# Squares of the activations taken from PSUM, a planner that costs one kind of matmul lower, and three small constants in one tile

## The chip, the core and the metric

The kernel runs on one core of one Trainium2 chip. The engines are named as in the profile: PE is TensorE's matmul (PEld its weight load), DVE is VectorE, ACT is ScalarE, POOL is GpSimd and SP is SyncE, whose queue issues nearly all DMAs. Each engine works through its own queue in order and waits there for semaphores of the others. The metric is the time on the device of one execution, in microseconds. Between the profiled execution's own time and the span that the profile shows from the first to the last instruction lie about two microseconds.

## What is computed

Two blocks with adaptive layer norm, over 2048 rows of 512 values, in float32. The first is a convolution of length 2048 for each of 512 channels, whose kernel comes from 128 complex poles; the second is a dense layer of 1792 units with a squared rectifier. Cut to what matters:

```python
def _A_ref(u, A_re, A_im, B_re, B_im, C_re, C_im, log_dt, Dskip):
    ...
    K = einsum("dn,dnl,dn->dl", Cc, exp(dt * A * l), dB).real
    y = irfft(rfft(pad(u)) * rfft(pad(K)))[:L] + u * Dskip
    return y

def _B_ref(x, w1, b1, w2, b2):
    h = x @ w1 + b1
    r = where(h > 0, h, 0)
    return (r * r) @ w2 + b2

mod = silu(c) @ w_mod                       # sa, ca, ga, sb, cb, gb
h = layernorm(x) * (1 + ca) + sa
x = x + ga * _A_ref(h, ...)
h = layernorm(x) * (1 + cb) + sb
x = x + gb * _B_ref(h, ...)
```

## The kernel before

It has two halves. Up to about 293 us, it makes the convolution in eight chunks of 64 channels: tables and transforms of the kernel, transforms of the input, products, and a first inverse step, whose result lies in the two big tiles `big0` and `big1`. After it come the second inverse step, the second layer norm and the dense layers.

**The second inverse step** (`inverse`, matmuls at L980) has four parts, n = 0 to 3, and each gives four tiles of 128 rows (s = 4n to 4n+3; tiles count from 0 to 15). A part has 256 small matmuls of 32 x 32 weights and 128 columns, as the profile counts them. Parts 0 and 2 write the two `tg` tiles of PSUM, parts 1 and 3 the four banks `ps0` to `ps2` and `kg`. Part 0 is emptied by DVE (L989), the others by ACT (L991), and for these POOL then adds the residual (L994).

**The layer norm** takes, for each tile, statistics on DVE (`statistics`: L1000, L1001), a square root on ACT (L1002), its reciprocal on DVE (L1003). `prepare` then scales the tile: for the first four tiles L1010 on DVE makes the negated mean times the reciprocal and L1012 on ACT scales, for the others L1014 on DVE does all of it. Four transposes on PE (L1021) put the tile into a bank, ACT (L1028, one quarter) and DVE (L1024, three quarters) modulate it, ACT (L1032) rounds it to the matmul's fast format and DVE or POOL (L1034) takes the rest, so that the sum of two rounded parts stands for the float32 value. L1017 and L1060 add the last bias to the residual on POOL.

**The dense layers** run over four groups of four tiles with 14 blocks of 128 units each, 56 steps in all. Step i has 12 matmuls of the first layer into one of the four banks (L1084, L1085, L1087: high by high, low by high, high by low) and 12 of the second layer of step i-2 into the `tg` tiles (L1104, L1105, L1106). Between them lie four instructions: the rectifier with its bias on ACT (L1090), the square on ACT, rounded (L1091), the square on DVE in full (L1092) and the difference of both (L1093), which is the low part. `w2_split` brings the second layer's weights, through two buffers of a quarter tile, and splits them (L929 on ACT, L930 on POOL).

**What sets the order.** The kernel is written down once, and `keep_order` then sets the order of every engine's queue: it runs the recorded instructions through a small model in which `weight` gives each a duration, takes on each engine the ready one with the longest way to the end, and fixes that order by dependencies. It models PE at half speed when the last window of 3413 ns was not busy enough (`level`), and lets DVE and POOL wait for each other where `shares_port` says that both use SBUF's shared port. So a change of one duration moves work in the second half, and the real times of the instructions don't change by it. The matmuls of inverse parts 0 and 1 and of the dense layers keep their written turn (`in_turn`); parts 2 and 3 and the first four tiles' transposes may move.

Of the kernel before, what the change touches and what calls it, by code (L numbers as in the profile page):

```python
# [11 lines left out]
F32 = mybir.dt.float32  # L12
FR = mybir.dt.float32r
I32 = mybir.dt.int32
AF = mybir.ActivationFunctionType
ALU = mybir.AluOpType
# [90 lines left out]
def weight(ins):  # L107
# [3 lines left out]
    if "DMA" in type(ins).__name__:  # L111
# [10 lines left out]
            if cols == 32 and ins.ins[1].ap[0][1] == 32:  # L122
                return 42, 42 + 130
            tiles = 128 // cols if cols in (32, 64, 128) else 1
# [28 lines left out]
def keep_order(tc, traced, slots, in_turn, whole, urgent, behind):  # L153
# [104 lines left out]
    for _ in groups:  # L258
# [7 lines left out]
        if e == "PE":  # L266
            kind = free_size(groups[g][0].ins[1]) if len(groups[g][0].ins) > 1 else shape
            cost += 0 if kind == shape else 230 if shape == 32 else 110
            shape = kind
            cost /= level(now)  # L270
            a = now
            while a < now + cost - 1:
                w = int(a // WINDOW)
                b = min(now + cost, (w + 1) * WINDOW)
                busy[w] = busy.get(w, 0) + b - a
                a = b
        elif e == "DVE":
            port = shares_port(groups[g][0])
            cost += max(0, free["Pool"] - now) if port else 0
        elif e == "Pool":  # L280
            cost += max(0, free["DVE"] - now) if port else 0
        elif e == "Activation":
            new = function_table(groups[g][0]) or table
            cost += 1283 if new != table else 0
            table = new
# [20 lines left out]
def tile_adaln_ssm_ffn(  # L306
# [60 lines left out]
    halfpi = ctile("halfpi", [P, 1])  # L367
    tiny = ctile("tiny", [P, 1])
    rsq = ctile("rsq", [P, 4])
    cin = ctile("cin", [P, 4])  # L370
# [78 lines left out]
    make_identity(nc, ident)  # L449
    pick, second = ctile("pick", [P, 128], FR), ctile("second", [P, 1])  # L450
    firsts = ident.rearrange("p (q a) -> p a q", q=4)
# [553 lines left out]
    def prepare(s):  # L1005
# [3 lines left out]
        if s < 4:  # L1009
            nc.vector.scalar_tensor_tensor(  # L1010
                mv[:, s, 1:2], mv[:, s, 0:1], -1.0, rstd2[:, s : s + 1], op0=ALU.mult, op1=ALU.mult)
            nc.scalar.activation(d4(xn), x2[:, s], AF.Identity, scale=rstd2[:, s : s + 1], bias=mv[:, s, 1:2])  # L1012
# [63 lines left out]
    def ffn1(i):  # L1076
# [14 lines left out]
        nc.scalar.activation(r2h, rr, AF.Square)  # L1091
        nc.vector.tensor_mul(rr, rr, rr)  # L1092
        nc.vector.tensor_sub(r2l, rr, r2h.bitcast(F32))  # L1093
        r2[i] = r2h, r2l
# [82 lines left out]
```

## Time and profile before

| | us |
|---|---|
| median of three runs | 655.47 |
| the three runs | 650.13, 655.47, 662.59 |
| the profiled execution, its own time | 654.19 |
| its span, first to last instruction | 652.1 |

| engine | busy us | share of the span |
|---|---|---|
| PE | 594.2 | 91% |
| PEld | 509.1 | 78% |
| DVE | 379.2 | 58% |
| ACT | 347.7 | 53% |
| POOL | 303.0 | 46% |

The mean granted clock of PE was 0.976 of full speed. On the chain of work that ended last, PE has 77% of the span, ACT 6%, DVE 5%, POOL 4%, waits that the profile cannot name 4%, and DMA 3%. These shares are means over the two halves, which have different limits: the first half uses all engines, the second is nearly PE alone. In the views below a row of the order of time has start, length, engine, line, operation, tiles, shape and count, and in brackets the idle time of the engine before it with what ended it. "issue" stands there where the engine waited for nothing that the profile shows. Rows that overlap were merged where they follow each other.

### The profile page before, as it was taken

How to read it: one execution, taken by the hardware profiler on the slowest of the kernel's cores; microseconds unless marked ns; L12 is line 12 of the kernel's file. 1: busy time of each engine (PE TensorE's matmuls, PEld its weight loads, DVE VectorE, ACT ScalarE, POOL GpSimd, SP SyncE). 2: the span in 40 equal slices, each digit the busy share in tenths (PEclk: the TensorE clock that was granted, in tenths of full speed). 3: DMA queues.
4: the chain of work that ended last, by engine and by line, in shares of the span. 5: the costliest groups of instructions: out<-in, count | busy, mean ns of one | idle time of the engine just before them, and what ended most of it. 6: DMA issues, size and time to landing. Idle time of an engine off the chain costs nothing.

```text
span 652.1 us, 20850 instructions
## 1 busy us (share of the span) xinstructions
PE 594.2 (91%) x9322; PEld 509.1 (78%) x9322; DVE 379.2 (58%) x646; ACT 347.7 (53%) x648; POOL 303.0 (46%) x251
## 2 busy tenths in 40 slices
PE   2389997999999999897769999999999999999995
PEld 2267886999899899885658888888888888888884
DVE  5797778899699789454596532533325332252223
ACT  4957999898997768433745532244322433222220
POOL 5489699999999996078976200011000100000000
PEclk9979999999999999997879999999999999999998
DMA  8932014032022405572141000100001000010001
GB/s 321 376 132 66 4 36 96 8 68 55 17 68 60 124 4 149 137 271 68 55 150 59 2 0 1 64 1 0 2 1 64 1 1 1 0 65 1 0 1 64
DMA packets 21705, 42.30 MB, mean 65 GB/s; under 512 B 3696, under 2 KB 9200, under 8 KB 20336
## 3 DMA queue, kind: packets, MB, share of 16 engines
q1 hardware_dynamic: 21184, 40.84, 20.3%
q8 instruction: 73, 1.20, 0.8%
q10 hardware_dynamic: 432, 0.14, 0.1%
q14 instruction: 16, 0.13, 0.1%
HBM read 28.39 MB, written 4.19 MB: 50 GB/s over the span
## 4 chain that ended last, share of the span: by engine, by line
PE 77%; ACT 6%; DVE 5%; POOL 4%; issue 4%; DMA 3%; SPq 0%; DVEq 0%; POOLq 0%; ACTq 0%
PE tg L1104 8%; PE tg L1105 8%; PE tg L1106 8%; PE ps L671 7%; PE ps L681 7%; PE ps L828 7%; PE ps L1085 6%; PE ps L1084 6%; PE ps L1087 6%; PE kg L809 4%; PE ps L634 3%; PE kg L1085 2%; PE kg L1084 2%; PE kg L1087 2%; ACT tables L756 1%
## 5 line engine op out<-in xcount | busy, mean ns | idle before, releaser
L1092 DVE TENSOR_TENSOR xy<-xy 128x512 f32<-128x512 f32 x56 | 45.8, 818 | 163.1 <-ACT rw L1091 106.4
L1090 ACT ACTIVATE xy<-ps,b1c 128x512 f32<-128x512 f32 x42 | 28.9, 689 | 134.5 <-PE ps L1087 134.5
L1017 POOL TENSOR_TENSOR big<-big,lo 128x512 f32<-128x512 f32 x12 | 16.0, 1332 | 158.5 <-DVE xy L1014 158.5
L681 PE MATMUL ps<-xy,t_sb 128*64 128x64 f32 x2048 | 66.7, 223 | 5.6 <-issue 3.3
L681 PEld LDWEIGHTS ps<-xy,t_sb 128*64 128x64 f32 x2048 | 63.5, 138 | 7.9 <-issue 3.6
L828 PE MATMUL ps<-e_sb,xy 128*64 128x128 f32 x1024 | 62.0, 274 | 2.8 <-issue 2.3
L828 PEld LDWEIGHTS ps<-e_sb,xy 128*64 128x64 f32 x1024 | 56.6, 138 | 4.7 <-issue 3.2
L673 ACT COPY xy<-ps 128x512 f32<-128x512 f32 x64 | 37.1, 591 | 15.3 <-PE ps L671 14.9
L789 POOL TENSOR_TENSOR rtl<-tables 128x1024 f32<-128x1024 f32 x22 | 43.4, 1971 | 0.2
L819 DVE TENSOR_TENSOR xy<-ps,xy 128x512 f32<-128x512 f32 x64 | 39.8, 680 | 2.0 <-PE ps L681 1.6
L1084 PE MATMUL ps<-h0h,w1h 128*128 128x512 f32 x88 | 35.3, 401 | 0.5 <-ACT big L991 0.5
L834 DVE COPY big<-ps 128x256 f32<-128x256 f32 x64 | 24.1, 417 | 19.8 <-PE ps L828 19.8
L765 POOL TENSOR_TENSOR llph<-lo,big 128x1024 int32<-128x1024 int32 x16 | 34.7, 2169 | 0.7 <-ACT tg L777 0.7
L765 POOL TENSOR_TENSOR rtl<-lo,big 128x1024 int32<-128x1024 int32 x16 | 34.3, 2142 | 1.5 <-ACT tg L777 1.0
L671 PE MATMUL ps<-d_sb,ksb 128*64 128x128 f32 x512 | 33.9, 275 | 1.1 <-DVE xy L819 0.8
L1090 ACT ACTIVATE xy<-kg,b1c 128x512 f32<-128x512 f32 x14 | 9.7, 690 | 47.1 <-PE kg L1087 42.8
L671 PE MATMUL ps<-d_sb,big 128*64 128x128 f32 x512 | 31.6, 274 | 0.8 <-ACT big L637 0.7
L1084 PE MATMUL ps<-h,w1h 128*128 128x512 f32 x80 | 31.6, 395 | 0.0
L1093 DVE TENSOR_TENSOR rw<-xy,rw 128x512 fp32r<-128x512 f32 x37 | 28.6, 774 | 2.9
L671 PEld LDWEIGHTS ps<-d_sb,ksb 128*64 128x64 f32 x512 | 28.1, 137 | 2.5 <-DVE xy L819 1.0
L671 PEld LDWEIGHTS ps<-d_sb,big 128*64 128x64 f32 x512 | 28.4, 137 | 1.6 <-ACT big L637 1.0
L800 DVE TENSOR_TENSOR rtl<-rtl,tg 128x1024 f32<-128x1024 f32 x22 | 26.7, 1213 | 2.4 <-POOL rtl L789 2.4
(260 smaller groups left out, 1604.0 us busy)
## 6 DMA issues: line engine op xcount, KB each, us to landing
xy<-xt SPq DMA_DIRECT2D x32, 256.0 KB, 4.4
xy<-xy SPq DMA_DIRECT2D x16, 512.0 KB, 6.2
xy<-w_mod SPq DMA_DIRECT2D x6, 1024.0 KB, 8.4
out_dram<-xy SPq DMA_DIRECT2D x16, 256.0 KB, 2.1
xy<-w SPq DMA_DIRECT2D x14, 256.0 KB, 3.1
raw<-w SPq DMA_DIRECT2D x6, 512.0 KB, 6.3
t_sb<-c_t SPq DMA_DIRECT2D x1, 2048.0 KB, 11.6
i2c<-c_i SPq DMA_DIRECT2D x1, 2048.0 KB, 8.5
```

The costliest lines, as they stand in the source:

```text
L671: nc.tensor.matmul(ps[64 * r : 64 * r + 64, 128 * i : 128 * i + 128], src[:, i], d1_sb[:, r], start=True, stop=True)
L681: nc.tensor.matmul(ps[64 * r : 64 * r + 64, 64 * i : 64 * i + 64].rearrange("p (h q t) -> p q h t", h=2, t=2), t2_sb[:, 8 * g + i, r], src ...
L765: nc.gpsimd.tensor_tensor(ph.rearrange("p d r (a b) -> p (d r) a b", a=4), bc(low_phase[:, us].rearrange("p d r b -> p (d r) b"), 2, 4), b ...
L789: nc.gpsimd.tensor_mul(am[:, 0, :, 32:96].rearrange("p d (v x) -> p d v x", v=2), bc(et[:, 256 + 8 * d0 : 384 + 8 * d0].rearrange("p (y a) ...
L828: nc.tensor.matmul(ps[64 * m : 64 * m + 64, 128 * i : 128 * i + 128], pairs(y)[:, g, i // 2, 64 * m : 64 * m + 64, i % 2], e1_sb[:, h], st ...
L1084: pe.append(nc.tensor.matmul(ps, w1h[:, q, fs], hh[:, q, :], start=(q == 0), stop=False))
L1085: pe.append(nc.tensor.matmul(ps, wl[:, q], hh[:, q, :], start=False, stop=False))
L1087: pe.append(nc.tensor.matmul(ps, w1h[:, q, fs], hl[:, q, :], start=False, stop=(q == 3)))
L1092: nc.vector.tensor_mul(rr, rr, rr)
L1104: pe.append(nc.tensor.matmul(acc, r2l[:, ms], hi_, start=(t == 0), stop=False))
L1105: pe.append(nc.tensor.matmul(acc, r2h[:, ms], lo_, start=False, stop=False))
L1106: pe.append(nc.tensor.matmul(acc, r2h[:, ms], hi_, start=False, stop=(t == NF - 1)))
```

## The change

Three things. Three small constants, of one, four and one columns, become views of one tile of eight columns, which moves the large tiles at the left side of SBUF by 64 bytes. In the dense layers, the square on DVE is taken as (bank + bias) times the rectified tile and written back into the bank in PSUM, and the low part is then the bank less the rounded square; before, it was the rectified tile times itself, in SBUF. In the planner, the small inverse matmul costs 24 ns instead of 42, and at least three quarters of the full clock are assumed for it. L1010 is written as one operation with two scalars, with the same result.

```diff
             if cols == 32 and ins.ins[1].ap[0][1] == 32:
-                return 42, 42 + 130
+                return 24, 24 + 130
...
-            cost /= level(now)
+            cost /= max(level(now), 0.75 if kind == 32 and groups[g][0].ins[1].ap[0][1] == 32 else 0)
...
-    tiny = ctile("tiny", [P, 1])
-    rsq = ctile("rsq", [P, 4])
+    small = ctile("small", [P, 8])
+    tiny, rsq, second = small[:, 0:1], small[:, 1:5], small[:, 5:6]
...
-    pick, second = ctile("pick", [P, 128], FR), ctile("second", [P, 1])
+    pick = ctile("pick", [P, 128], FR)
...
-            nc.vector.scalar_tensor_tensor(
-                mv[:, s, 1:2], mv[:, s, 0:1], -1.0, rstd2[:, s : s + 1], op0=ALU.mult, op1=ALU.mult)
+            nc.vector.tensor_scalar(
+                mv[:, s, 1:2], mv[:, s, 0:1], rstd2[:, s : s + 1], -1.0, op0=ALU.mult, op1=ALU.mult)
...
-        nc.vector.tensor_mul(rr, rr, rr)
-        nc.vector.tensor_sub(r2l, rr, r2h.bitcast(F32))
+        nc.vector.scalar_tensor_tensor(ps, ps, b1c[:, t : t + 1], rr, op0=ALU.add, op1=ALU.mult)
+        nc.vector.tensor_sub(r2l, ps, r2h.bitcast(F32))
```

The order of every engine stays as it was up to the second inverse step. Behind it, three places matter. In the names, the numbers behind the tiles only count tiles and differ between the two programs; `ps_160` of before is `ps_158` of after, `big_84` and `big_85` are `big_83` and `big_84`.

PE, from the end of inverse part 1 to the start of part 3. Before (a quarter of part 2 is four rows, eight matmuls in each):

```order
L980 MATMUL tg_427<-big_85,i2c 32x128 x8
L980 MATMUL tg_428<-big_85,i2c 32x128 x8
L1021 MATMUL ps_160<-ident,xy_92 128x128 x4
L1021 MATMUL ps_161<-ident,xy_92 128x128 x4
L980 MATMUL tg_427<-big_84,i2c 32x128 x8
L980 MATMUL tg_428<-big_84,i2c 32x128 x8
L980 MATMUL tg_427<-big_85,i2c 32x128 x8
L980 MATMUL tg_428<-big_85,i2c 32x128 x8
L1021 MATMUL kg_364<-ident,xy_92 128x128 x4
L1021 MATMUL ps_159<-ident,xy_92 128x128 x4
```

Two quarters of part 2 follow there, and then part 3. After, the end of part 2:

```order
L980 MATMUL tg_425<-big_84,i2c 32x128 x8
L980 MATMUL tg_426<-big_84,i2c 32x128 x8
L1021 MATMUL ps_158<-ident,xy_91 128x128 x4
L1021 MATMUL ps_159<-ident,xy_91 128x128 x4
L1021 MATMUL kg_362<-ident,xy_91 128x128 x4
L1021 MATMUL ps_157<-ident,xy_91 128x128 x4
L980 MATMUL ps_157<-big_83,i2c 32x128 x4
```

The four tiles' transposes moved behind all of part 2, and part 3 follows them at once.

ACT, at the same place: the root L1002 and scaling L1012 of the first four tiles, and the copies L991 of part 1. Before:

```order
L929 CAST w_5030<-xy_96 128x512
L1002 ACTIVATE rstd_77<-mv_72,epsb 128x1
L1012 ACTIVATE xy_92<-big_84,mv_72,rstd_77 128x512
L1002 ACTIVATE rstd_77<-mv_72,epsb 128x1 x2
L991 COPY big_84<-ps_160 128x4x8x16
```

After:

```order
L991 COPY big_83<-ps_158 128x4x8x16
L1002 ACTIVATE rstd_76<-mv_71,epsb 128x1
L991 COPY big_83<-ps_159 128x4x8x16
L1002 ACTIVATE rstd_76<-mv_71,epsb 128x1
L991 COPY big_83<-kg_362 128x4x8x16
L1012 ACTIVATE xy_91<-big_83,mv_71,rstd_76 128x512 x2
L1002 ACTIVATE rstd_76<-mv_71,epsb 128x1 x2
L991 COPY big_83<-ps_157 128x4x8x16
L1012 ACTIVATE xy_91<-big_83,mv_71,rstd_76 128x512 x2
```

The copies of part 1 moved ahead of the first root, and the splitting of two weight tiles (L929) moved behind this stretch. Further on, the copies of part 3 now stand behind the roots of tiles 5 to 7.

POOL, from the end of the first layer's weights to the second layer's. Before:

```order
L930 TENSOR_TENSOR w_5020<-xy_96,w_5020 128x512
L930 TENSOR_TENSOR w_5030<-xy_96,w_5030 128x512
L1060 TENSOR_TENSOR big_84<-big_84,lo 128x4x8x16 x4
L994 TENSOR_TENSOR big_84<-big_84,xy_94 128x4x8x16 x2
L1034 TENSOR_TENSOR h0l<-xy_92,h0h 128x4x128 x4
L930 TENSOR_TENSOR w_5030<-xy_96,w_5030 128x512 x2
L994 TENSOR_TENSOR big_84<-big_84,xy_94 128x4x8x16 x4
```

After:

```order
L1060 TENSOR_TENSOR big_83<-big_83,lo 128x4x8x16 x2
L994 TENSOR_TENSOR big_83<-big_83,xy_93 128x4x8x16 x4
L1034 TENSOR_TENSOR h0l<-xy_91,h0h 128x4x128 x4
L930 TENSOR_TENSOR w_5018<-xy_95,w_5018 128x512
L930 TENSOR_TENSOR w_5028<-xy_95,w_5028 128x512
L994 TENSOR_TENSOR big_83<-big_83,xy_93 128x4x8x16 x3
```

The residual adds of tiles 4 to 7 moved ahead of L1034, two weight splits and two L1060 moved behind. On DVE, the first square L1092 stands behind the statistics of tile 10, where before it stood behind those of tile 9.

## The prediction

> **What bounds the kernel now.** I read the tenths of the page first, then the sums of PE's waits around the place that the tenths show, then the order of time there. The tenths:
>
> ```profile
> PE   2389997999999999897769999999999999999995
> POOL 5489699999999996078976200011000100000000
> PEclk9979999999999999997879999999999999999998
> ```
>
> PE, the TensorE matmul, is at 9 from the sixth slice on, and from slice 23 (358 us) without a break: the feed-forward part has no wait to give. The one weak place is slices 19 to 21, 293 to 342 us, where PE falls to 7, 6 and 9 and its granted clock to 7, 8 and 7. PE's waits between 290 and 345 us:
>
> ```profile
> PE tg L1104 <- DVE w1lc L1093: 5.7, 1, 5.7
> PE tg L980 <- issue: 2.7, 3, 1.5
> ```
>
> From 345 us on there is no wait of PE in the trace at all. The longest is one wait of 5.7 us, of the first second-layer matmul for the low half of the first square. In order of time:
>
> ```profile
> 329.81 3.77 POOL L994 TENSOR_TENSOR big<-big,xy 128x512 f32<-128x512 f32 x3
> 329.87 6.69 DVE L1092 TENSOR_TENSOR xy<-xy 128x512 f32<-128x512 f32 x1 [0.33 <-ACT w1lc L1091]
> 330.57 1.08 PE L1087 MATMUL kg<-h0l,w1h 128*128 128x512 f32 x4
> 334.71 1.30 POOL L994 TENSOR_TENSOR big<-big,xy 128x512 f32<-128x512 f32 x1
> 336.59 0.69 DVE L1093 TENSOR_TENSOR w1lc<-xy,w1lc 128x512 fp32r<-128x512 f32 x1
> 337.34 0.79 PE L1104 MATMUL tg<-w,w1lc 128*128 128x512 f32 x1 [5.69 <-DVE w1lc L1093]
> ```
>
> The square on DVE takes 6.69 us instead of some 0.68 (its row has two SBUF operands), and ends 0.55 us after POOL's last add of that run (334.71 + 1.30 = 336.01). So it stood behind POOL. PE was done at 331.65 and waits until 337.34. It then starts at half speed:
>
> ```profile
> 336.00:338.00 2.00, 0.66 (x2) 0.57 (x3) 1.86 (x4) 0.62 (x1) 0.01 (x1) 0.50 0.35 127
> 338.00:340.00 2.00, 2.00 (x6) 1.58 (x5) 1.89 (x3) 1.72 (x4) 0.69 (x1) 0.50 0.00 0
> 340.00:342.00 2.00, 2.00 (x8) 1.58 (x7) 1.97 (x5) 0.00 (x0) 2.00 (x2) 0.70 0.16 24
> 342.00:344.00 2.00, 2.00 (x10) 1.66 (x9) 0.62 (x2) 0.00 (x0) 2.00 (x3) 1.00 0.35 120
> ```
>
> The third number from the end is the granted clock. 0.70 over 340 to 342 is 0.50 until 341.2, so PE runs at half speed from 337.34 to 341.2, 3.9 us, and loses 1.9 us of work.
>
> **Part 1, the square.** 56 times the product on DVE reads the PSUM bank (plus the bias) and the rectified tile, and writes the bank; the difference at L1093 reads the bank. Rows of both kinds with one PSUM operand:
>
> ```profile
> L819 DVE TENSOR_TENSOR xy<-ps,xy x64: 677/679/695, 104.6 to 283.2; 128x512 f32<-128x512 f32 x64
> L627 DVE SCALAR_TENSOR_TENSOR xy<-xy,mv,kg x16: 716/734/742, 34.1 to 48.6; 128x512 f32<-128x512 f32 x16
> ```
>
> L819 ran 64 times between 104 and 283 us, where POOL is mostly at 9 in the tenths, and none took over 695 ns. So an operand in PSUM frees the instruction from POOL. Writing PSUM from DVE has no row. I take 0.73 us from L627, which is nearest (three operands, one in PSUM). The bounds are 0.68 (L819) and twice 0.73; even that hides in the feed-forward part, where PE is busy all of the time and DVE less than two fifths:
>
> ```profile
> 450.00:500.00 50.00, 50.00 (x222) 41.00 (x221) 18.80 (x29) 16.17 (x28) 2.58 (x2) 1.00 0.03 12
> ```
>
>  The Trainium skill, "SBUF — State Buffer", Who interferes with whom, says that a DVE instruction with at most one SBUF input, outside the 2-port modes, does not contend with GpSimd, and one with two does; the 695 ns against 6.69 us agree, and the sum by it is the same.
>
> The wait of 5.69 us then goes if the first square is ready when PE has done its three first-layer groups. That is worked out below, since the order of the work ahead moves too. With the wait goes the half speed behind it, 1.9 us, for PE then has no idle stretch. Sum of part 1: -7.6 us. Costs at nothing: a bank is now held until L1093, about 0.7 + 0.7 us longer, but four banks rotate and one first-layer group plus one second-layer group last 24 matmuls, 5.5 us (10 in 2.00 us and a little less in the rows above); the cover is two such steps. The wait of DVE for the bank's other users adds nobody, since the relu has waited for the same matmuls.
>
> **Part 2, the planner.** The third inverse (L980, tg banks) now runs in one piece, behind it the 16 transposes L1021, and behind these the fourth inverse. PE's rows:
>
> ```profile
> 295.66 1.93 PE L980 MATMUL tg<-big,i2c 32*32 32x128 f32 x128 [0.58 <-issue]
> 299.13 0.72 PE L980 MATMUL tg<-big,i2c 32*32 32x128 f32 x34 [1.54 <-issue]
> ...
> 306.61 0.42 PE L980 MATMUL kg<-big,i2c 32*32 32x128 f32 x1 [0.89 <-issue]
> ...
> 308.80 1.88 PE L1021 MATMUL ps<-ident,xy 128*128 128x128 f32 x8
> ...
> 312.69 0.66 PE L1021 MATMUL ps<-ident,xy 128*128 128x128 f32 x4 [0.43 <-ACT big L991]
> 313.28 1.90 PE L980 MATMUL tg<-big,i2c 32*32 32x128 f32 x128
> 317.10 0.42 PE L980 MATMUL ps<-big,i2c 32*32 32x128 f32 x12 [1.91 <-DVE xy L1024]
> ```
>
> ```profile
> 295.00:300.00 5.00, 2.88 (x199) 2.29 (x196) 0.27 (x1) 0.00 (x0) 5.00 (x4) 1.00 0.12 24
> ```
>
> PE needs 1.93 us for 128 of these small matmuls, yet starts the next 128 3.47 us later (299.13), and the 256 behind these take 7.48 (to 306.61), with "issue" waits in between: their instructions arrive no faster than 128 in 3.5 to 3.75 us, though the DMA engines are busy only 0.12 of the time around the longest gap. In before, the transposes and the wait for L1024 lie in that time. Unbroken, the third inverse pays it: the piece of 306.61 holds 34 matmuls of the second inverse and 94 of the third; the next starts at 310.1 to 310.4, the next at 313.6 to 314.2, and its 34 at 15 to 25 ns end at 314.1 to 315.0. Then the transposes begin. What follows is the same chain as before, later:
>
> ```profile
> 312.54 0.81 ACT L1028 ACTIVATE xy<-ps,sbc,cbc 128x128 f32<-128x128 f32 x2
> 313.04 2.00 DVE L1024 TENSOR_SCALAR xy<-ps,cbc,sbc 128x128 f32<-128x128 f32 x6 [1.72 <-ACT xy L1028]
> 315.91 1.04 DVE L1024 TENSOR_SCALAR xy<-ps,cbc,sbc 128x128 f32<-128x128 f32 x3
> ```
>
> Four transposes 0.66, the scaling on ACT 0.47 (two pitched into 0.81), and DVE's twelve, 313.04 to 316.95, 3.91: they start at 315.2 to 316.1 instead of 313.04. So the fourth inverse, and the feed-forward part behind it, start 2.2 to 3.1 us later. I take 2.6, the middle, and with the fourth inverse as long as before the first-layer matmul moves from 323.10 to 325.7. As DVE now has BN_STATS of tile 4 ahead of L1024, and that waits for POOL's first L994 (313.9, from the count below; 0.69 more), 314.6 is the earliest start whatever PE does: the lower bound of this term is 1.5. The Trainium skill, "Runtime: NRT & Kernel Launch", Instruction fetch mechanics, calls the crossing of a 16 KiB block of 256 instructions mostly hidden. The gaps of 0.58 to 1.54 us after each 128 matmuls (each with its weight load) speak against it here; by it the sum would take the lower bound, as in the third rival.
>
> **Is the first square ready?** POOL now has 13 instructions ahead of the statistics of tile 10 (they count from 0), which stand ahead of the first square on DVE. Rows for their size, and for the one DVE instruction in that stretch that still has only SBUF operands:
>
> ```profile
> 307.44 0.59 ACT L991 COPY big<-ps 128x512 f32<-128x512 f32 x1 [0.92 <-PE ps L980]
> 307.92 0.81 ACT L1012 ACTIVATE xy<-big,mv,rstd 128x512 f32<-128x512 f32 x1
> 308.63 0.57 ACT L991 COPY big<-ps 128x512 f32<-128x512 f32 x1
> 308.81 2.49 POOL L1060 TENSOR_TENSOR big<-big,lo 128x512 f32<-128x512 f32 x2 [1.28 <-ACT xy L1012]
> 315.93 5.15 POOL L1034 TENSOR_TENSOR h0l<-xy,h0h 128x512 fp32r<-128x512 f32 x4
> 318.51 1.44 DVE L1014 TENSOR_SCALAR xy<-big,mv,rstd 128x512 f32<-128x512 f32 x1
> 321.04 2.51 POOL L930 TENSOR_TENSOR w<-xy,w 128x512 fp32r<-128x512 f32 x2
> 323.50 5.09 POOL L994 TENSOR_TENSOR big<-big,xy 128x512 f32<-128x512 f32 x4
> ```
>
> POOL's take 1.27 each. ACT now begins with the second inverse's copies at 307.44; a copy follows the last by 0.48, a scaling by 0.71, a root by some 0.2, so the first scaling stands behind three copies and two roots, 309.3 to 310.1, and the two L1060 that wait for it end 2.5 later, at 312.6. The 13 end at 329.1. Then statistics and root, together 1.2, the relu 0.69, product 0.73 and difference 0.69: 332.4. PE needs it 8.55 us (323.10 to 331.65) after its start, at 334.2. So there are 1.8 us to spare, and no new wait.
>
> **Part 3.** One tile for the small constants moves every large tile at the left by 64 bytes; the order and the waits of the first 290 us stay. L1010, four instructions on one element, changes its form and no longer precedes what PE waits for. Both at nothing, covered by the wait for the third inverse.
>
> **Sum.** -5.69 - 1.9 + 2.6 = -5.0 us on the profiled execution, 654.19 us around a span of 652.1: 649.2. The median of the three runs, 655.47, lies 1.3 above that execution and would come to 650.5. I predict 650.
>
> **The rivals.**
> - The wait moves ahead of the feed-forward part: slower. L1014 of tile 4 stands on DVE at about 320.8, in the middle of POOL's row without a pause, and ACT now empties the fourth inverse's banks only behind the square roots of tiles 5 to 7, which need DVE's statistics behind L1014. At 318.51 L1014 took 1.44 us, one change of POOL's instruction; the square at 329.87 was passed over at five. Held until POOL pauses at 329.1, L1014 ends at 329.7, and statistics, root and copy (2.2 us) let PE start at 331.9, 8.8 late, at half speed: 652.1 + 8.8 - 5.7 = 655.2, a run of 657.3. It decides from about six passed instructions on, at 1.25 us each. Chance 0.12.
> - The change does not do what it says: the product still waits for POOL, since the rectified tile is in SBUF. Only the cost of part 2 stays: 654.19 + 2.6 = 656.8. L819's 695 ns speaks against it; that it writes SBUF and this one PSUM leaves a chance of 0.13.
> - The third inverse runs without gaps, because instructions come faster there than in the two inverses ahead of it: it then ends at 312.5 and the lower bound of 1.5 holds, 654.19 - 7.6 + 1.5 = 648.1. Against it: the gap of 1.54 us came with the DMA engines nearly idle, so it was no matter of load. Chance 0.12.
> - My forecast has 0.63.
>
> **How the numbers follow.** The range takes in the first two rivals nearly whole and the other cost bounds: 646 (term of part 2 at 1.5, less two us for runs that differ) to 657. A gain or loss of 2%, about what a measurement of this kernel can tell from no change, is 13 us: 642.4 and 668.6. The three runs spread from 5.3 below to 7.1 above their median. A median 7 us under my forecast is left one time in ten, and as often for the third rival's: 0.09 faster. The slow rivals lack 11 us to the other bound: 0.04. Within 2%: 0.87.
>
> **What the profile after would show.** L1104's first wait gone or under 1 us, and the clock full from 326 us on; L1092 at 0.70 to 0.75 us with no long ones; the first L1084 at 325 to 326.5; two "issue" waits inside the third inverse and L980's wait for L1024 at 2 us or more. Wrong it would be if L1014 or an L1092 stands for several us, if the first L1084 comes before 324, or if PE waits in the feed-forward part for a bank.

## The result, and the profile after

| | before | changed |
|---|---|---|
| median of 20 runs, us | 651.57 | 647.02 |
| lowest and highest, us | 646.89, 662.59 | 642.09, 653.56 |

The ratio is 0.9927 with a 95% interval of 0.9906 to 0.9949: the changed kernel is faster by 0.7%, some 4.8 us, which is inside the 2% that counts as no change. The prediction said 650, 646 to 657.

The execution of the changed kernel that was profiled first was a slow one (653.56 us), so the rows below are from a second execution of the same kernel (647.88 us, span 646.1). Its tenths:

```profile
PE   2499997999999999896799999999999999999995
POOL 6489799999999996066699200001000100000000
PEclk9999999999999999898679999999999999999998
```

PE still falls to 6 and 7 in slices 19 and 20, 291 to 323 us, and its clock to 8, 6 and 7 in slices 19 to 21: the weak place is shorter, not gone. What PE waited for between 290 and 345 us (total, times, longest):

```profile
PE tg L980 <- issue: 3.8, 4, 1.5
PE kg L980 <- issue: 3.3, 2, 2.6
PE ps L980 <- DVE mv L1001: 2.3, 1, 2.3
PE ps L980 <- issue: 0.7, 1, 0.7
PE ps L1084 <- ACT big L991: 0.5, 1, 0.5
```

The wait of L1104 for the first square, 5.7 us before, is not in the list. From 345 us on PE waits for nothing, as before. The squares on DVE (count, shortest, median and longest in ns):

```profile
L1092 DVE SCALAR_TENSOR_TENSOR ps<-ps,b1c,xy x42: 728/759/759, 332.5 to 632.0; 128x512 f32<-128x512 f32 x42
L1092 DVE SCALAR_TENSOR_TENSOR kg<-kg,b1c,xy x14: 727/759/759, 340.2 to 626.6; 128x512 f32<-128x512 f32 x14
```

Not one of the 56 took longer than 759 ns. The first five lie wholly within POOL's busy time, and these show that POOL does not hold them; the others met no instruction of POOL. One sign that the prediction named for being wrong did come: L1014 of tile 5 stood for several us (3.98 here, 3.88 in the first profile), while that of tile 4 took 1.08 in both. It cost PE nothing.

```profile
345.74 3.98 DVE L1014 TENSOR_SCALAR xy<-big,mv,rstd 128x512 f32<-128x512 f32 x1 [0.51 <-PE ps L1021]
```

In order of time on PE, from the last block of the third inverse to the first second-layer matmul:

```profile
312.96 1.06 PE L980 MATMUL tg<-big,i2c 32*32 32x128 f32 x34 [0.89 <-issue]
313.95 1.97 PE L1021 MATMUL ps<-ident,xy 128*128 128x128 f32 x8
...
316.57 1.06 PE L1021 MATMUL ps<-ident,xy 128*128 128x128 f32 x4
319.94 0.37 PE L980 MATMUL ps<-big,i2c 32*32 32x128 f32 x12 [2.31 <-DVE mv L1001]
...
326.21 0.80 PE L1084 MATMUL ps<-h0h,w1h 128*128 128x512 f32 x1 [0.54 <-ACT big L991]
...
336.94 0.39 PE L1104 MATMUL tg<-w,w1lc 128*128 128x512 f32 x1
```

The third inverse is one piece, the transposes stand behind it, and L1104 follows without a wait. (The 2.31 us are the wait that the prediction put down to L1024; L1001 is the statistic right behind the last L1024.) But from the first L1084 to it pass 10.73 us, where the profile of before had 8.55 without its wait (14.24 - 5.69). The stretches of two us say why; the granted clock is the third number from the end:

```profile
324.00:326.00 2.00, 1.42 (x53) 0.85 (x52) 0.39 (x4) 0.72 (x2) 2.00 (x3) 0.50 0.03 8
326.00:328.00 2.00, 1.79 (x4) 1.50 (x5) 0.00 (x0) 1.63 (x4) 2.00 (x2) 0.50 0.52 138
328.00:330.00 2.00, 2.00 (x6) 1.53 (x5) 1.49 (x3) 0.80 (x2) 2.00 (x3) 0.50 0.66 179
330.00:332.00 2.00, 2.00 (x7) 1.54 (x7) 1.29 (x7) 1.21 (x4) 2.00 (x3) 0.63 0.76 221
332.00:334.00 2.00, 2.00 (x11) 1.65 (x10) 1.48 (x3) 1.09 (x2) 2.00 (x2) 1.00 0.76 221
```

Here the dense layers begin at half clock and get the full one only at about 331.5. In the first profile of before they began at the full one:

```profile
322.00:324.00 2.00, 1.46 (x39) 1.05 (x24) 0.00 (x0) 1.54 (x4) 2.00 (x3) 1.00 0.35 81
324.00:326.00 2.00, 2.00 (x11) 1.63 (x10) 0.88 (x2) 0.73 (x4) 2.00 (x2) 1.00 0.23 67
```

It is not the change's doing alone: of the 14 profiles in the table below, 12 run 3.4 to 6.0 us at the start of the dense layers at half clock, the second profile of before among them.

The table has the marks from which all that follows is read, for every profile taken: the starts of the first L980, L1084 and L1104, the span, the differences of neighbours, and the wait of the first L1104 (all us). The ratio to the kernel before is from the timed runs.

| kernel | L980 | L1084 | L1104 | span | L980 to L1084 | L1084 to L1104 (wait in it) | L1104 to end | ratio |
|---|---|---|---|---|---|---|---|---|
| before | 293.62 | 323.10 | 337.34 | 652.13 | 29.48 | 14.24 (5.69) | 314.80 | 1 |
| before, second profile | 297.67 | 326.34 | 338.88 | 653.47 | 28.67 | 12.54 (2.42) | 314.60 | |
| changed | 299.47 | 331.51 | 342.62 | 651.77 | 32.05 | 11.11 (0) | 309.14 | 0.9927 |
| changed, second profile | 292.80 | 326.21 | 336.94 | 646.10 | 33.41 | 10.73 (0) | 309.16 | |
| square alone | 296.32 | 326.18 | 336.13 | 649.09 | 29.86 | 9.96 (0) | 312.95 | 0.9948 |
| planner alone | 299.47 | 332.26 | 348.94 | 663.24 | 32.79 | 16.68 (5.40) | 314.30 | 1.0135 |
| constants and L1010 | 293.44 | 323.91 | 334.11 | 643.29 | 30.47 | 10.21 (0) | 309.18 | 0.9890 |
| changed without planner | 294.00 | 323.75 | 332.04 | 641.19 | 29.75 | 8.30 (0) | 309.15 | 0.9870 |
| constants alone | 292.67 | 323.08 | 336.91 | 647.76 | 30.40 | 13.83 (3.79) | 310.86 | 0.9942 |
| L1010 alone | 294.74 | 325.25 | 335.52 | 648.58 | 30.50 | 10.27 (0) | 313.07 | 0.9973 |
| square, right side moved | 295.38 | 325.39 | 335.42 | 649.55 | 30.01 | 10.03 (0) | 314.13 | 0.9979 |
| without planner, left by 32 bytes | 294.61 | 325.39 | 336.15 | 650.76 | 30.78 | 10.76 (0) | 314.61 | 0.9969 |
| without planner, both sides moved | 294.21 | 328.45 | 338.45 | 647.47 | 34.23 | 10.00 (0) | 309.02 | 0.9872 |
| third inverse twice | 297.86 | 337.75 | 348.20 | 657.35 | 39.89 | 10.45 (0) | 309.15 | |

Two things are to be seen at once. The first L980 comes anywhere between 292.7 and 299.5, with no change of order ahead of it, so a single span says little and the differences behind it more. And the stretch from the first L1104 to the end has two values: 309.0 to 309.2 in six profiles, 312.9 to 314.8 in seven (and 310.86 once, with half clock behind a wait).

### The profile page after: what moved, and what is told of

Its sections match the earlier page's. It is cut to its first block, busy times and chain, and to the rows that moved or that the text cites. A ratio compares the mean times of both kernels' runs of the same rounds, so it can differ in the third digit from the quotient of the medians.

```text
span 651.8 us, 20880 instructions
## 1 busy us (share of the span) xinstructions
PE 594.2 (91%) x9322; PEld 512.7 (79%) x9322; DVE 376.2 (58%) x646; ACT 348.2 (53%) x648; POOL 301.4 (46%) x251
## 4 chain that ended last, share of the span: by engine, by line
PE 69%; issue 3%; ACT 3%; DVE 2%; DVEq 0%; ACTq 0%
PE tg L1106 8%; PE tg L1104 8%; PE tg L1105 8%; PE ps L1084 6%; PE ps L1085 6%; PE ps L681 6%; PE ps L1087 6%; PE ps L828 6%; PE ps L671 4%; PE kg L809 3%; PE kg L1084 2%; PE kg L1085 2%; PE kg L1087 2%; PE tg L980 1%; PE ps L980 1%
## 5 line engine op out<-in xcount | busy, mean ns | idle before, releaser
L1092 DVE SCALAR_TENSOR_TENSOR ps<-ps,b1c,xy 128x512 f32<-128x512 f32 x42 | 31.8, 757 | 112.2 <-ACT xy L1090 112.2
L681 PE MATMUL ps<-xy,t_sb 128*64 128x64 f32 x2048 | 68.7, 226 | 9.9 <-issue 4.5
L681 PEld LDWEIGHTS ps<-xy,t_sb 128*64 128x64 f32 x2048 | 65.2, 141 | 12.7 <-issue 5.1
L1084 PE MATMUL ps<-h0h,w1h 128*128 128x512 f32 x88 | 36.2, 412 | 0.5 <-ACT big L991 0.5
L1084 PE MATMUL ps<-h,w1h 128*128 128x512 f32 x80 | 31.4, 393 | 0.0
L1092 DVE SCALAR_TENSOR_TENSOR kg<-kg,b1c,xy 128x512 f32<-128x512 f32 x14 | 10.6, 755 | 35.5 <-ACT xy L1090 35.5
```

Of the source, the lines that this page charges most:

```text
L681: nc.tensor.matmul(ps[64 * r : 64 * r + 64, 64 * i : 64 * i + 64].rearrange("p (h q t) -> p q h t", h=2, t=2), t2_sb[:, 8 * g + i, r], src ...
L1084: pe.append(nc.tensor.matmul(ps, w1h[:, q, fs], hh[:, q, :], start=(q == 0), stop=False))
L1092: nc.vector.scalar_tensor_tensor(ps, ps, b1c[:, t : t + 1], rr, op0=ALU.add, op1=ALU.mult)
```

## The experiments

**The square alone.** The diff's two lines L1092 and L1093, the rest as before.

```diff
-        nc.vector.tensor_mul(rr, rr, rr)
-        nc.vector.tensor_sub(r2l, rr, r2h.bitcast(F32))
+        nc.vector.scalar_tensor_tensor(ps, ps, b1c[:, t : t + 1], rr, op0=ALU.add, op1=ALU.mult)
+        nc.vector.tensor_sub(r2l, ps, r2h.bitcast(F32))
```

> The kernel before with the square alone: L1092 reads PSUM and writes PSUM, L1093 reads PSUM; the planner's numbers and the constants stay as before. The order of PE is that of before, word for word. My theory (the gain is the freed square, the cost is the planner's): the first second-layer matmul no longer waits (5.7 us) and the half clock behind it (1.9 us) goes, so 7.6 us under the kernel before, a ratio of 0.988, and about 3 us under the changed kernel; the first L1084 stays at 323 us. Rival, the gain is the new order's: 0 to -2 us. Rival, a product that writes PSUM still waits for POOL: 0.

Measured: 0.9948 (0.9918 to 0.9978), 3.4 us; by the ratios that is some 1.4 us over the changed kernel, not 3 under it. The planner takes the new square for one that does not share the port, so the orders of DVE, ACT and POOL move too, but only behind the first square. The wait is gone in the profile, and from the first L1104 to the end it is 1.85 us shorter than before: the half clock behind the wait went too. In time it gives less than half of the 7.6 us. All 56 squares took 727 to 760 ns, six of them wholly within POOL's busy time, which rules out the rival of a product that still waits; why it gains so little is taken up with the second profile of before.

**The planner alone.** The square keeps its two SBUF operands.

```diff
-                return 42, 42 + 130
+                return 24, 24 + 130
...
-            cost /= level(now)
+            cost /= max(level(now), 0.75 if kind == 32 and groups[g][0].ins[1].ap[0][1] == 32 else 0)
```

> The kernel before with the planner's two numbers alone (24 for 42, and the floor of 0.75); the square keeps its two SBUF operands. My theory, terms that add up: +2.6 us (the third inverse without the transposes in between), and the wait of the first second-layer matmul stays near 5.7 us; a ratio of 1.004. Since POOL's row has no pause behind the first square in this order, the wait can also be longer, up to some 10 us (1.015). Rival, the new order is where the gain comes from: -2 to -5 us. Rival, the old wait hides the later start: 0.

Measured: 1.0135 (1.0096 to 1.0174), 8.8 us slower. From the first L980 to the first L1084 it takes 3.3 us more than the profile of before, and the wait stays:

```profile
340.84 7.33 DVE L1092 TENSOR_TENSOR xy<-xy 128x512 f32<-128x512 f32 x1
348.94 0.79 PE L1104 MATMUL tg<-w,w1lc 128*128 128x512 f32 x1 [5.40 <-DVE w1lc L1093]
```

The new order is a loss by itself; with the freed square it costs less (below). The sum of the two alone is a loss, and both together a gain.

**The constants and L1010.**

```diff
-    tiny = ctile("tiny", [P, 1])
-    rsq = ctile("rsq", [P, 4])
+    small = ctile("small", [P, 8])
+    tiny, rsq, second = small[:, 0:1], small[:, 1:5], small[:, 5:6]
...
-            nc.vector.scalar_tensor_tensor(
-                mv[:, s, 1:2], mv[:, s, 0:1], -1.0, rstd2[:, s : s + 1], op0=ALU.mult, op1=ALU.mult)
+            nc.vector.tensor_scalar(
+                mv[:, s, 1:2], mv[:, s, 0:1], rstd2[:, s : s + 1], -1.0, op0=ALU.mult, op1=ALU.mult)
```

> The kernel before with the constants in one tile and the other form of L1010 alone; the order on all engines is that of before. My theory: 0, a ratio of 0.998 to 1.002. Rival, the 64 bytes by which the big tiles stood elsewhere matter: over 1 us either way.

Measured: 0.9890 (0.9835 to 0.9946), 7.2 us faster, twice as much as the square. My "at nothing" falls. In the profile two things differ: the first L1104 no longer waits, though the square has its old form, and the stretch from L1104 to the end is 309.18 against 314.80.

**The changed kernel without the planner's numbers.** The same two lines of the planner put back.

```diff
-                return 24, 24 + 130
+                return 42, 42 + 130
...
-            cost /= max(level(now), 0.75 if kind == 32 and groups[g][0].ins[1].ap[0][1] == 32 else 0)
+            cost /= level(now)
```

> The changed kernel with the planner's numbers put back (42, no floor): the square and the constants together. My theory: the same as the square alone, 7.6 us under before (0.988) and about 3 us under the changed kernel, with the first L1084 at 323 us against 325.7 at the same start of the inverse. Rival, the order does not matter since its gaps are the same instruction supply in another place: the same time as the changed kernel (0.993).

Measured: 0.9870 (0.9829 to 0.9910), 8.5 us under before. That is near the ratio expected (0.988), but not for the reason given, that it would be that of the square alone, which was 0.9948. Against the constants and L1010 alone (0.9890) the square adds little, and the intervals do not part the two. By the two ratios it is some 3.7 us under the changed kernel; these two intervals just overlap, and the kernels were not timed against each other. In the profile the first L1084 comes 2.3 to 3.7 us sooner behind the first L980 than in the changed kernel, and the dense layers start at full clock: 8.30 us from L1084 to L1104, the shortest of all.

**The constants alone, and L1010 alone.** To the kernel before, first only this:

```diff
-    tiny = ctile("tiny", [P, 1])
-    rsq = ctile("rsq", [P, 4])
+    small = ctile("small", [P, 8])
+    tiny, rsq, second = small[:, 0:1], small[:, 1:5], small[:, 5:6]
```

> The kernel before with the constants in one tile alone (L1010 as before). What it tells apart: in the runs so far the start-to-start step of two 512-column matmuls in the feed-forward part is 226 to 227 ns with the constants in one tile and 229 to 235 ns without, which over 1344 matmuls is 3.3 us. New theory (the address of the left-hand tiles sets the step): the step is 226 to 227 ns and the part behind the first second-layer matmul lasts 309 us; the first square still waits behind POOL, since L1010 is as before; 3 to 5 us under before. Rival (L1010's form is the cause): the step stays at 229 to 235 ns and the time at that of before.

And only this:

```diff
-            nc.vector.scalar_tensor_tensor(
-                mv[:, s, 1:2], mv[:, s, 0:1], -1.0, rstd2[:, s : s + 1], op0=ALU.mult, op1=ALU.mult)
+            nc.vector.tensor_scalar(
+                mv[:, s, 1:2], mv[:, s, 0:1], rstd2[:, s : s + 1], -1.0, op0=ALU.mult, op1=ALU.mult)
```

> The kernel before with L1010's other form alone (constants as before). New theory: the step stays at 229 to 235 ns; L1010 no longer waits for POOL (three times 0.5 to 0.8 us on DVE), POOL's row comes about 1 us earlier, a pause opens in it and the first square gets in after two of POOL's instructions, as in the run with both, so that most of the 7.6 us of the wait and the half clock goes: 4 to 7 us under before. Rival (the address shift let the square in): the wait of 5 us or more stays, and the time is that of before.

Measured: constants 0.9942 (0.9900 to 0.9984), L1010 0.9973 (0.9943 to 1.0003). In the one profile of each they part. With the constants alone the square is held as in before, and the wait is there:

```profile
329.41 6.72 DVE L1092 TENSOR_TENSOR xy<-xy 128x512 f32<-128x512 f32 x1 [0.35 <-ACT w1lc L1091]
336.91 0.80 PE L1104 MATMUL tg<-w,w1lc 128*128 128x512 f32 x1 [3.79 <-DVE w1lc L1093]
```

With L1010 alone POOL's row is ahead of ACT's L929 at 334 us, pauses for it, and the square gets in at that pause, after 3.20 us:

```profile
330.37 3.81 POOL L994 TENSOR_TENSOR big<-big,xy 128x512 f32<-128x512 f32 x3
331.53 3.20 DVE L1092 TENSOR_TENSOR xy<-xy 128x512 f32<-128x512 f32 x1 [1.45 <-ACT w1lc L1091]
334.84 1.78 POOL L930 TENSOR_TENSOR rw<-xy,rw 128x512 fp32r<-128x512 f32 x1 [0.66 <-ACT rw L929]
```

So the wait went with L1010's form, and the step of the matmuls with the addresses. How the form does it is argued from these rows and not shown: in its new form L1010 took 212 to 215 ns in every profile, in the old one up to 1120, POOL comes to its pause sooner, and the square gets in. The order of the three kernels (before, constants alone, L1010 alone) is the same, and the wait of before itself was 5.69 us in one execution and 2.42 in another (below). The 4 to 7 us expected of L1010 did not show in the time (1.8 us, -0.2 to 3.7). Its profile does not promise them either: from the first L980 to the end it took 353.84 us, 2.0 and 4.7 less than the two profiles of before.

The step, from the start of one matmul to the start of the next, shows in the mean duration of one matmul (the last number before the second bar, ns). In the second profile of before, 400 to 600 us, a pair of tiles from both sides of SBUF, another such, and a pair of the right-hand side:

```profile
L1104 PE MATMUL tg<-w,w1lc 128*128 128x512 f32 x24 | 9.5, 396 | 0.0
L1087 PE MATMUL ps<-h0l,w1h 128*128 128x512 f32 x48 | 13.1, 394 | 0.0
L1104 PE MATMUL tg<-w,rw 128*128 128x512 f32 x41 | 16.0, 390 | 0.0
```

The same three in the changed kernel:

```profile
L1104 PE MATMUL tg<-w,w1lc 128*128 128x512 f32 x24 | 9.3, 389 | 0.0
L1087 PE MATMUL ps<-h0l,w1h 128*128 128x512 f32 x44 | 11.8, 390 | 0.0
L1104 PE MATMUL tg<-w,rw 128*128 128x512 f32 x47 | 18.3, 389 | 0.0
```

In before, `w` and `w1h` lie at the right and `w1lc` and `h0l` at the left; pairs across take 4 to 7 ns longer, pairs of one side nearly the same. That points at the places of the two tiles that one matmul reads, weights and columns. The next matmul counts too: in the trace of the square alone, a matmul with both tiles at the right steps 227 ns (median of 451) when those of the next one lie there as well, and 231 (of 116) when the next one's weights lie at the left. In the program of before, the left-hand tiles start 32 bytes past a multiple of 512 and the right-hand ones 480; the 64 bytes of the constants put the left at 480 too.

**The right side moved, and the left by 32 bytes.** To the square alone, 64 bytes at the top of the right-hand stack:

```diff
-    ub = tc.alloc_tile_pool(name="ub", bufs=1, side="right")
+    ur = tc.alloc_tile_pool(name="ur", bufs=1, side="right"); right = ur.tile([P, 16], F32, tag="right", name="right"); ub = tc.alloc_tile_pool(name="ub", bufs=1, side="right")
...
-    ub.release()
+    ub.release(); ur.release()
```

> The kernel with the square alone, and 64 bytes more at the top of the right-hand stack, so that the tiles of both sides lie 32 bytes past a multiple of 128 (with the square alone: 32 on the left, 96 on the right; in the changed kernel 96 on both). The order is that of the square alone. Theory (what counts is that the tiles that PE reads at one time lie alike): the step falls to 226 to 227 ns and the time by 3.3 us against the square alone. Rival (32 past a multiple of 128 is bad in itself): the step stays at 229 ns or grows to 233, the time is the same or 2 us longer.

To the changed kernel without the planner's numbers, a longer constants tile:

```diff
-    small = ctile("small", [P, 8])
+    small = ctile("small", [P, 16])
```

> The changed kernel without the planner's numbers, its constants tile 32 bytes longer: left-hand tiles at a multiple of 128 bytes, right-hand tiles 96 past one. Theory (alike or not): the step is 229 to 235 ns, 3 to 4 us over the kernel without this. Rival (only 32 past a multiple is bad, or a multiple of 128 is good): 226 to 227 ns and the same time. Which of the two holds on the left side alone cannot be told by the first runs, which had only 32 and 96.

Measured: 0.9979 (0.9944 to 1.0014) and 0.9969 (0.9930 to 1.0009). With the right side moved, the step stays long:

```profile
L1087 PE MATMUL ps<-h0l,w1h 128*128 128x512 f32 x44 | 12.0, 395 | 0.0
L1104 PE MATMUL tg<-w,w1lc 128*128 128x512 f32 x24 | 9.5, 396 | 0.0
```

Alike modulo 128 is not enough: that theory falls. The rival falls with the other kernel, whose left-hand tiles are not 32 past a multiple of 128 and which is slow. The left by 32 bytes, which leaves the order word for word, takes 314.61 us from L1104 to the end instead of 309.15, and with it most of the gain of its kernel.

**Both sides moved.** The changed kernel without the planner's numbers; two more constants in the one tile, and the 64 bytes at the right.

```diff
-    unmagic = ctile("unmagic", [P, 1])
-    epsb = ctile("epsb", [P, 1])
...
-    tiny, rsq, second = small[:, 0:1], small[:, 1:5], small[:, 5:6]
+    tiny, rsq, second, unmagic, epsb = small[:, 0:1], small[:, 1:5], small[:, 5:6], small[:, 6:7], small[:, 7:8]
...
-    ub = tc.alloc_tile_pool(name="ub", bufs=1, side="right")
+    ur = tc.alloc_tile_pool(name="ur", bufs=1, side="right"); right = ur.tile([P, 16], F32, tag="right", name="right"); ub = tc.alloc_tile_pool(name="ub", bufs=1, side="right")
...
-    ub.release()
+    ub.release(); ur.release()
```

> The changed kernel without the planner's numbers, both sides 64 bytes lower: two more constants move into the one tile, and 64 bytes lie at the top of the right-hand stack. Left-hand and right-hand tiles then both start 416 bytes past a multiple of 512 (the changed kernel: both 480; before: 32 and 480; with the right side moved alone: 32 and 416). Theory (the two sides have to lie alike modulo 512, which the moved right side missed by 128): 226 to 227 ns, the part behind the first second-layer matmul 309 us, the time that of the kernel without the planner's numbers, 0.987 of before. Rival (480 past a multiple of 512 is good in itself): 229 to 235 ns, 313 us, 0.993.

Measured: 0.9872 (0.9827 to 0.9918), 309.02 us from L1104 to the end, and in the groups of matmuls:

```profile
L1087 PE MATMUL ps<-h0l,w1h 128*128 128x512 f32 x46 | 12.4, 389 | 0.0
L1104 PE MATMUL tg<-w,w1lc 128*128 128x512 f32 x24 | 9.3, 389 | 0.0
```

So no address is good in itself: both sides at 480 and both at 416 are fast, 32 with 480, 0 with 480 and 32 with 416 slow. Alike modulo 512 is enough, alike modulo 128 is not; 256 was not tried.

This profile also shows a rival of the prediction that did not come in the changed kernel, L1014 of tile 4 held by POOL while PE waits for it:

```profile
314.94 4.98 POOL L1034 TENSOR_TENSOR h0l<-xy,h0h 128x512 fp32r<-128x512 f32 x4
317.52 9.98 DVE L1014 TENSOR_SCALAR xy<-big,mv,rstd 128x512 f32<-128x512 f32 x1
319.86 2.51 POOL L930 TENSOR_TENSOR w<-xy,w 128x512 fp32r<-128x512 f32 x2
322.30 4.91 POOL L994 TENSOR_TENSOR big<-big,xy 128x512 f32<-128x512 f32 x4
327.63 0.29 ACT L1002 ACTIVATE rstd<-mv,small 128x1 f32<-128x1 f32 x1 [8.60 <-DVE mv L1001]
328.45 0.80 PE L1084 MATMUL ps<-h0h,w1h 128*128 128x512 f32 x1 [5.10 <-ACT big L991]
```

L1014 gets in only when POOL's row ends at 327.2; the root waits for the statistics behind it, the last copy for the root, and the first L1084 comes 5.10 us late. In the same order with other addresses (the kernel without the planner's numbers) L1014 was held for 0.9 us.

**Second profiles.** Both kernels once more, nothing edited.

> The kernel before once more, for a second profile. The runs so far give the square less in time (3.4 us) than its terms in one profile (7.6 us). Theory (the wait is a fixed matter of the order): the first square is passed over at 5 POOL instructions again, the first second-layer matmul waits 4 to 6 us and starts at half clock, and the stretch from the first inverse matmul to the end lasts 357 to 359 us. Rival (the profile before was an unlucky execution): the wait is under 3 us and the stretch under 355 us.

> The changed kernel once more, for a profile of an execution that was not disturbed. Theory: from the first inverse matmul to the first L1084 32 us (2.3 over the kernel without the planner's numbers), then no wait of the first L1104, and 309.1 us from there to the end; the first inverse matmul at 293 to 296 us and not 299.5, so a span of 645 us. Rival (the order itself makes the first half later): the first inverse matmul at 299 us again and a span near 651.

Measured for before, 655.43 us:

```profile
332.74 3.84 POOL L994 TENSOR_TENSOR big<-big,xy 128x512 f32<-128x512 f32 x3
332.84 4.28 DVE L1092 TENSOR_TENSOR xy<-xy 128x512 f32<-128x512 f32 x1 [0.36 <-ACT w1lc L1091]
336.50 1.77 POOL L930 TENSOR_TENSOR rw<-xy,rw 128x512 fp32r<-128x512 f32 x1
337.15 1.67 DVE L1093 TENSOR_TENSOR w1lc<-xy,w1lc 128x512 fp32r<-128x512 f32 x1
338.88 0.50 PE L1104 MATMUL tg<-w,w1lc 128*128 128x512 f32 x1 [2.42 <-DVE w1lc L1093]
```

The same square in the same order stood behind three of POOL's instructions, not five, and got in without a pause in POOL's row: L930 had to wait for it (1.77 us instead of some 1.30). PE waited 2.42 us, not 5.69. So the 5.69 us were a matter of that execution, not of the order. PE also came to the wait later: from L1084 to L1104 it took 10.12 us without the wait instead of 8.55, since here too the dense layers began at half clock:

```profile
326.00:328.00 2.00, 1.66 (x4) 1.38 (x5) 0.16 (x1) 1.75 (x4) 2.00 (x3) 0.60 0.51 131
328.00:330.00 2.00, 2.00 (x6) 1.55 (x6) 1.62 (x5) 0.80 (x2) 2.00 (x2) 0.55 0.35 126
```

The wait is as the rival had it; the stretch lies between the two forecasts. From the first L980 to the end it took 355.80 us, against 358.51 in the first profile and 352.77 with the square alone: 3.0 to 5.7 us, where the runs gave 3.4 (1.4 to 5.4).

The changed kernel took 647.88 us and has been shown. Its first L980 came at 292.80, so the change does not force the 299.47 of its first profile. Still, three of the four profiles with the planner's numbers have it at 297.86 or later, and one of the ten others (297.67); why was not followed up.

**The third inverse twice.** Its matmuls are issued a second time into the same banks and give the same sums.

```diff
-            for r in range(2):
+            for r in (0, 1, 0, 1) if n == 2 else (0, 1):
```

> The changed kernel with the third inverse issued twice into the same banks, 256 more small matmuls as the profile counts them. Theory (the instructions arrive no faster than 128 in 3.5 to 3.75 us): two more blocks, so from the first inverse matmul to the first L1084 4.7 to 7.5 us more than in the changed kernel (32.05), the lower end if the wait for L1024 takes some of it. Rival (it is PE's own time, 15 ns each): at most 3.9 us more, and 1.6 if that wait takes some. In the inverses the blocks of 128 start 3.4 to 3.75 us apart by the theory and 2 us apart by the rival.

Measured, 659.13 us: from the first L980 to the first L1084 6.5 and 7.8 us more than in the changed kernel's two profiles (the forecast was 4.7 to 7.5 against the first of these, where it was 7.8). The blocks of 128, in order of time:

```profile
311.12 0.42 PE L980 MATMUL kg<-big,i2c 32*32 32x128 f32 x1 [1.16 <-issue]
...
315.13 2.84 PE L980 MATMUL tg<-big,i2c 32*32 32x128 f32 x128 [1.12 <-issue]
319.13 1.05 PE L980 MATMUL tg<-big,i2c 32*32 32x128 f32 x34 [1.17 <-issue]
```

They start 4.0 us apart, each behind an "issue" wait, and PE is done with one in 2.84 us (at half clock). The stretch with the wait at 310 us:

```profile
310.00:312.00 2.00, 0.88 (x44) 0.73 (x54) 0.00 (x0) 0.06 (x1) 0.00 (x0) 0.50 0.00 0
```

The clock is 0.50, DVE and POOL stand still, and the DMA share is 0.00. Two blocks at PE's own pace would be 5.7 us; the rest is "issue" wait. The rival's steps of 2 us are not there, but it was priced at full clock, and of the 6.5 to 7.8 us most would also be there at half clock without a wait. What the trace shows is the wait itself, and its place: counted in PE's matmuls, the five "issue" waits between 302 and 320 us stand exactly 128 apart, and one block ahead of the first of them there is none. That it is the instructions that come late is inferred from this; the profile names nothing. The Trainium skill, "Runtime: NRT & Kernel Launch", Instruction fetch mechanics, holds the step to the next block of instructions mostly hidden; for matmuls this short these rows do not agree.

## Why the prediction was right, and where it was not

The time (647.0 for 650) and the side were right, and the sum was near: -5.0 us forecast, -4.55 between the medians, -4.4 between the means of the two profiles of each kernel, from the first L980 to the end (357.2 and 352.8). By stretches, in these means, it is +3.7 up to the first L1084, -2.5 from there to the first L1104 and -5.6 behind it. The terms were not near: four of them were off and the errors cancelled, so that the sum came out well by luck. The three runs shown before lay 3.9 us above the median of twenty, which is why the figure came out high. The prediction also misread PE's tenths: from 293 to 342 us they are 7, 7 and 6, not 7, 6 and 9, and slices 7 and 17 are below 9; nothing in the sum hangs on that.

- **The freed square, -5.69.** The mechanism held: an operand in PSUM frees the square from POOL, 727 to 759 ns for all 56, and the first L1104 does not wait. The rival that it still waits (0.13) is out. The size was that of one execution. The wait was 5.69 and 2.42 in two profiles, 4.1 in the mean; the interval of the square alone, 1.4 to 5.4 us, takes that in. How much of it is the square's in the changed kernel is not settled, since with L1010's new form PE did not wait for the old square either (0 in both profiles).
- **The half clock behind the wait, -1.9.** The half clock behind L1104 went (314.7 in the mean, 312.95 with the square alone). But "PE then has no idle stretch" failed, and so did "the clock full from 326 us on", by 5 us: the changed kernel starts the dense layers at 0.50, and from L1084 to L1104 it takes 11.11 and 10.73 us, where the sum had 8.55. I had looked only at PE's idle time behind the inverse step, and the clock was low from that step on, which is full of waits. The price came from the one profile of before that began at full clock; its second took 10.12 without its wait, the square alone 9.96, and only the kernel without the planner's numbers 8.30. So part of this loss is in before as well: the first 6.0 and 5.3 us are at half clock in the changed kernel, 3.4 in the second profile of before. What decides it was not tested.
- **The planner, +2.6.** Right in sign and place: two "issue" waits inside the third inverse that before does not have are there (0.84 and 0.89 us, 0.56 and 0.61 in the first profile), and so are the 2.31 us ahead of the fourth. The size is 3.7: 29.1 in the mean of before, 32.7 of the changed kernel, from L980 to L1084. The sum had taken PE's pieces at full clock, and they ran at half: 1.06 us for the last 34 instead of 0.5 to 0.85, and 1.7 from the first transpose to DVE's L1024 instead of 1.1. Over that whole stretch the changed kernel is at half clock for 21.3 and 22.0 us, before for 13.7 and 10.2. The rival of an inverse without gaps (0.12) is out. As the planner alone it costs 8.8 us by the runs and 6.6 in its profile: 3.7 ahead of L1084, and 3.3 from there to L1104, where the old square keeps its wait (5.40).
- **Constants and L1010, 0.** This step was wrong: "both at nothing" looked for a change in the order and the waits and found none. The 64 bytes change no order but the step of every matmul in the dense layers: 312.95 us with the square alone, 309.15 with the constants too, 3.8 us, or 2.9 ns for each of some 1300 matmuls. It is the surest gain of the change: the seven profiles with alike addresses all have it.
- **L1014 held behind POOL (0.12).** For tile 4, the one that the rival priced, not in the changed kernel's profiles, where it took 1.08 us both times. But the mechanism is real: tile 5's took 3.88 and 3.98 us there, at a place where PE does not wait, and with both sides moved tile 4's took 9.98 us and PE lost 5.10, where the rival had priced 8.8.
- **The cover of the dense layers** held: no wait of PE from 345 us on, the bank is free in time.

What is left open: when DVE gets in between two of POOL's instructions. The first square stood behind two, three, five and six of them, in the order of before behind two, three and five; L1014 behind one and eight in the same order. What sorts these was not found. Nor was it found what makes the dense layers begin at half clock, nor why the two sides have to lie alike. Of the kernels tried, the changed one without the planner's numbers has the lowest ratio, 0.9870.

## What to carry to other kernels

A wait in one profile that hangs on two engines meeting at a port should be priced from two or three executions, not from one. Where a change moves tiles, look at the step of a steady row of matmuls as well as at waits: a per cent there (3.8 us) was worth about as much here as the one long wait (2.4 to 5.7 us). A removed wait need not give back the clock: look at the granted clock of the whole stretch ahead of it, and in more than one execution.

## What the runs showed of the hardware that was not expected

- **A matmul's step hangs on where its two tiles lie.** In the dense layers at full clock, 512 columns step at 227 ns in the mean when the weights' and the columns' tiles start alike modulo 512 bytes (480 and 480, 416 and 416), and at 230 to 231 otherwise (230.0 for 32 and 480, 231.4 for 0 and 480, 230.9 for 32 and 416). The Trainium skill, "SBUF — State Buffer", SBUF: two separate sides, says that among the engines only the port shared by DVE and GpSimd makes anyone wait, and PE never; here PE is 1.2% slower by an address alone. Why was not found, nor whether it then waits for anyone.
- **DVE can be passed over many times.** L1014 of tile 4 took 9.98 us behind eight of POOL's instructions in a row, and 1.08 in the changed kernel, whose next one took 3.98 behind three.
- **Short matmuls wait at every 128.** In the inverses, blocks of 128 were 3.5 to 4.8 us apart, with 0.6 to 2.7 us of "issue" wait ahead of nearly each.
